# Attention ahead of two expert stages: a chunk's gate products from GpSimd to ScalarE, and a conversion's four small DMAs one step later

## The chip, the cores and the metric

The kernel runs on one core of one Trainium2 chip. The metric is the device time of one execution in microseconds (us); the kernel before took 919.73 us, the median of three runs (919.49 to 921.26). Engines are named as the profile names them: PE (TensorE matmul), PEld (its weight load), DVE (VectorE), ACT (ScalarE), POOL (GpSimd) and SP (SyncE, which here only issues DMAs). PEq, SPq and ACTq are the queues of PE, SP and ACT.

## What is computed

The program computes a gated linear attention, sends its output through a layer of eight experts with a fixed capacity, and that through a gated product with a third weight. The change lies in the attention, whose reference is, cut short:

```python
for t in range(S):                       # S = 768, B = 4, H = 8, D = 40
    m_new = np.maximum(f_gate[:, :, t] + m, i_gate[:, :, t])
    f_stab = np.exp(f_gate[:, :, t] + m - m_new)
    i_stab = np.exp(i_gate[:, :, t] - m_new)
    m = m_new
    C = f_stab * C + i_stab * outer(vt, kt)
    n = f_stab * n + i_stab * kt
    h_tilde = C @ qt
    y[:, :, t] = sigmoid(o_gate[:, :, t]) * h_tilde / max(abs(n . qt), 1)
x = y.transpose(0, 2, 1, 3).reshape(B * S, H * D)
x = moe(x)                               # 8 experts, 384 tokens each
out = (x @ w_a * (x @ w_b)) @ w_out
```

## The kernel before

The attention works in chunks of T = 128 tokens: NC = 6 chunks (c) by B = 4 batches (b) make 24 steps, n = 4c + b. In a step the queries and keys of eight heads are multiplied (`pq`, L392), and the result is weighted by a 128 x 128 matrix of decays per head. That matrix comes from one matmul per four heads, `pe` (L384): its stationary operand is `est[:, b]` (a row of the gates, kept only on the partitions of batch b) and its moving operand is `mov` (another row of the gates, kept only on the partitions of a head). ACT takes the exponential of `pe` into `dd` (L386), POOL clears what lies above the diagonal (L387, a select), DVE multiplies `pq` by `dd` into `P` (L395), and PE multiplies `P` by the values into `pv` (L423). POOL later forms `x` from numerator, denominator and output gate (L460, L462), PE transposes it (`px`, L472) and takes the routing logits (`pl`, L482). Everything is one program per engine, each in the order in which it was written: the function `attention` interleaves the pieces of neighbouring steps by hand, with generators. `s1(n + 1)` (the pe, dd, P part of the next step) runs inside step n; `pe` has one PSUM buffer, so the second half's `pe` waits for the first half's `dd`.

`gates(c)` makes a chunk's gate rows, and is run in small portions by `fill` during the chunk before (each `yield` ends a portion; after `yield "w"` the next generator in the list has its turn). In its last part POOL forms `mov` in two halves of four heads (L323, 128 x 512 each) and `est` in one (L332, 128 x 512), all as products of a row with a 0/1 column per head or batch, `hsel` and `bsel`. The first chunk has its own branch, before the loop. A step n is counted here by PE's time, from its first `pe` of `s1(n + 1)` to the next. By it the products of chunks 2 to 5 run in steps 5, 9, 13 and 17 (`mov` first half and `est`; the program writes them at the end of the step before) and in steps 6, 10, 14 and 18 (`mov` second half); those of chunk 1 run in step 2.

Beside the attention runs `conv`: 13 pieces of the last stage's weights are decoded from 64-bit words on DVE (`mu`, L119, L122, L125) and ACT (`mq`, `msg`), split into a high part on ACT (`wh` L131, `mth` L133, `woh` L148) and a low part on POOL (`wl` L134, `mtl` L136, `wol` L149). DVE's next piece waits for the low part, as `mu` has one buffer. A piece of kind "f" (nine of the 13) ends with four small DMAs on SP, from `mth` and `mtl` into `wh` (L139, L140). The function `fin` of a piece is put into a list and run by `flush`, once a step; DMAs that `self.dma` puts off (`x`'s store, the output gate's load) and the raw weights' loads are issued by `drain`, right after `flush`.

SP issues the loads of the step after next at the head of each step: four of `qr` (L263, L264; three buffers, so the load waits until the matmul `pg`, L408, of the step before has read the buffer) and one of `vk` (L266). Its queue is in order: a DMA that waits holds back all behind it.

Of the kernel before, what the change touches and what calls it, by code (L numbers as in the profile page):

```python
# [6 lines left out]
F32 = mybir.dt.float32  # L7
# [7 lines left out]
AF = mybir.ActivationFunctionType  # L15
# [5 lines left out]
B, H, S, D = 4, 8, 768, 40  # L21
# [22 lines left out]
class Kern:  # L44
# [68 lines left out]
    def conv(self, pool, kind, i, raw, more, nxt):  # L113
        nc = self.nc
        V, P, A = nc.vector, nc.gpsimd, nc.scalar
        words = raw.bitcast(I32).rearrange("p (n two) -> p n two", two=2)
        qi, sg = self.cva
        u = pool.tile([128, CW], I32, tag="ot", name="mu", bufs=1)
        V.tensor_scalar(u, words[:, :, 1], 3, None, op0=OP.logical_shift_left)  # L119
        more()  # L120
        yield 0.5
        V.tensor_tensor(u, u, qi, op=OP.add)  # L122
        yield 0.8
        F = u.bitcast(F32)
        V.tensor_tensor(F, F, sg, op=OP.mult)  # L125
        if kind == "f":
            h, l = self.wh[i], self.wl[i]
            n4, c4 = slice(0, 512), slice(512, 640)

            def fin():  # L130
                A.activation(h[:, 0:4].rearrange("p a b -> p (a b)"), F[:, n4], AF.Copy)  # L131
                th, tl = [pool.tile([128, 128], F32R, name=n, bufs=1) for n in ("mth", "mtl")]
                A.activation(th, F[:, c4], AF.Copy)  # L133
                P.tensor_sub(l.rearrange("p a b -> p (a b)"), F[:, n4],  # L134
                             h[:, 0:4].rearrange("p a b -> p (a b)").bitcast(F32))
                P.tensor_sub(tl, F[:, c4], th.bitcast(F32))  # L136
                for s in range(2):
                    r = slice(64 * s, 64 * s + 64)
                    nc.sync.dma_start(h[0:64, 4 + s].bitcast(F32), th[r].bitcast(F32))  # L139
                    nc.sync.dma_start(h[64:128, 4 + s].bitcast(F32), tl[r].bitcast(F32))  # L140
                nxt()

            yield from self.later(fin)
        else:
            h = self.woh[i].rearrange("p a b -> p (a b)")

            def fin():
                A.activation(h, F, AF.Copy)  # L148
                P.tensor_sub(self.wol[i].rearrange("p a b -> p (a b)"), F, h.bitcast(F32))  # L149
                nxt()  # L150

            yield from self.later(fin)
        self.done.add((kind, i))
# [60 lines left out]
    def attention(self, es):  # L214
        tc, nc, a = self.tc, self.nc, self.a
# [18 lines left out]
        hsel = gs[:, 6:14]  # L234
        dsel = gs[:, 14:30]
        psel = gs[:, 30:158]
        bsel = gs[:, 158:162]
# [36 lines left out]
        def sig(c):  # L274
            nc.scalar.activation(SG[c], SG[c], AF.Sigmoid)
            nc.scalar.activation(warm, gs[0:1, 0:1], AF.Exp)

        def gates(c):
            t = FI.pop(c)
            fg, ig = t[:, 0], t[:, 1]  # L280
            mt = wk.tile([128, 1 + T], F32, name="mt")
            if c:
                nc.vector.tensor_copy(mt[:, 0:1], MT[c - 1][:, T:])
            else:
                nc.vector.memset(mt[:, 0:1], -1e30)
            MT[c] = mt
            mc, mp = mt[:, 1:], mt[:, 0:T]
            yield 0
            nc.vector.tensor_tensor_scan(mc, fg, ig, mp[:, 0:1], op0=OP.add, op1=OP.max)
            yield 0  # L290
            lf = wk.tile([128, T], F32, name="lf", bufs=1)
            nc.vector.tensor_add(lf, fg, mp)
            yield 0
            nc.vector.tensor_sub(lf, lf, mc)
            if c == 0:
                nc.vector.memset(lf[:, 0:1], 0.0)
            yield 0
            cc = wk.tile([128, T], F32, name="cc", bufs=1)
            nc.vector.tensor_sub(cc, ig, mc)
            A = wk.tile([128, T], F32, name="A", bufs=1)  # L300
            nc.vector.tensor_tensor_scan(A, self.ones, lf, 0.0, op0=OP.mult, op1=OP.add)
            yield 0
            zs = wk.tile([128, 2, T], F32, name="zs", bufs=1)
            nc.vector.tensor_scalar(zs[:, 1], A, za, oa, op0=OP.mult, op1=OP.add)
            nc.vector.tensor_sub(cc, cc, A)
            yield 0
            nc.vector.tensor_scalar(zs[:, 0], cc, zc, oc, op0=OP.mult, op1=OP.add)
            hi = wk.tile([128, 2, T], F32R, name="hi", bufs=1)
            EW = wk.tile([128, 2, T], F32, name="EW", bufs=1)

            def fin():
                nc.scalar.activation(hi, zs, AF.Copy)
                nc.scalar.activation(EW[:, 0], A, AF.Exp)
                nc.scalar.activation(EW[:, 1], cc, AF.Exp, bias=A[:, T - 1:T])

            yield from self.later(fin, False)
            ar = wk.tile([128, T], F32, name="ar", bufs=1)
            nc.vector.scalar_tensor_tensor(ar, hi[:, 1].bitcast(F32), b2, zs[:, 1], op0=OP.mult, op1=OP.add)
            mov = wk.tile([128, H, T], F32R, name="mov")

            def half(g):
                e = nc.vector if c == 0 and g else nc.gpsimd
                e.tensor_tensor(mov[:, 4 * g:4 * g + 4], ar[:, None, :].to_broadcast([128, 4, T]),  # L323
                                hsel[:, 4 * g:4 * g + 4, None].to_broadcast([128, 4, T]), op=OP.mult)

            half(0)
            es1 = wk.tile([128, T], F32, name="es1", bufs=1)
            nc.vector.scalar_tensor_tensor(es1, hi[:, 0].bitcast(F32), b1, zs[:, 0], op0=OP.mult, op1=OP.add)
            est = wk.tile([128, B, T], F32R, name="est")

            def spread(e, b0, b1_):
                e.tensor_tensor(est[:, b0:b1_], es1[:, None, :].to_broadcast([128, b1_ - b0, T]),  # L332
                                bsel[:, b0:b1_, None].to_broadcast([128, b1_ - b0, T]), op=OP.mult)

            if c == 0:
                spread(nc.vector, 0, 1)
            else:
                spread(nc.gpsimd, 0, B)
            yield 0
            md = wk.tile([128, 16], F32, name="md", bufs=1)  # L340
            nc.vector.tensor_scalar(md, dsel, EW[:, 0, T - 1:T], None, op0=OP.mult)
            yield 0
            for _ in range(4):
                yield "w"
            half(1)
            if c == 0:
                spread(nc.gpsimd, 1, B)
            GA[c] = (est, mov, EW, md)
            yield 0

# [171 lines left out]
        for n in range(NS):  # L522
            c, b = divmod(n, B)
            if n == 2:
                bg.append(m2)
            if True:
                if n + 2 < NS:
                    load(n + 2)
                if n == 1:
                    next(m2)  # L530
                if b == 3 and c + 1 < NC:
                    gates2(c + 1)
                    if c + 2 < NC:
                        bg.insert(0, gates(c + 2))
                        if c + 3 < NC:
                            load_g(c + 3)
                m = s1(n + 1) if n + 1 < NS else iter(())
                next(m, None)
                g = s2g(n)
                next(g, None)  # L540
                fill(2)
                next(m, None)
                next(m, None)
                if n == 0:
                    sig(0)
                if b == 3 and c + 1 < NC:
                    sig(c + 1)
                self.flush(b < 3)
                self.drain()
                next(g, None)  # L550
                next(m, None)
                if n + 1 < NS:
                    pre(n + 1)
                g = s2(n)
                next(g)
                if 0 <= n - 2:
                    s3(n - 2)
                next(g)
                lc = s4(n - 3) if n >= 3 else lambda: None
                fill(2)  # L560
                next(g)
                fill(1)
                next(g)
                fill(1)
                next(g, None)
                lc()
            if n:
                xout(n - 1)
                if n % B == 0 and n // B + 1 < NC:
                    load_o(n // B + 1)  # L570
            if n - 3 == 7 or n - 3 == 15:
                bg.insert(0, self.keys(*KT[(n - 3) // 8]))
            fill(1)
# [643 lines left out]
```

## Time and profile before

| | us |
|---|---|
| median of three runs | 919.73 |
| the profiled execution | 922.35 |
| its span, first to last instruction | 920.6 |
| busy in the span: PE / PEld | 830.0 / 786.8 |
| busy in the span: DVE / POOL / ACT | 543.8 / 433.6 / 337.0 |

The profiled execution took 2.6 us more than the median. A row of a timeline gives the start, the duration, the engine, the line, the operation, the tile written and those read, and in brackets how long the engine was idle just before and what ended that. A releaser is inferred: it is the last thing that ended before the wait did. A mean share over the whole span says little here, since the attention (the first 212 us) and the two expert stages after it have different limits.

### The profile page before, as it was taken

The page shows a single profiled execution, that of the slowest core. Times are in us where ns is not written, and L with a number is a line of the kernel's source. Part 1 is how long each engine was busy: PE and PEld are TensorE (multiplying, and loading weights), DVE is VectorE, ACT ScalarE, POOL GpSimd, SP SyncE. Part 2 cuts the span into 40 slices and gives each one's busy share as a digit, 9 for nine tenths or more (in the row PEclk, how much of TensorE's full clock was granted, in tenths as well). Part 3 has the DMA queues.
Part 4 walks back from the last instruction along what each step waited for, and adds up shares of the span by engine and source line. Part 5 has one row for each costly group of instructions (what it writes and reads, how often), then busy time and mean ns, then how long its engine had stood idle before and what let it go on. Part 6 is the DMA issues. An engine that isn't in the chain of part 4 may idle for free.

```text
span 920.6 us, 15838 instructions
## 1 busy us (share of the span) xinstructions
PE 830.0 (90%) x5939; PEld 786.8 (85%) x5939; DVE 543.8 (59%) x1188; ACT 337.0 (37%) x660; POOL 433.6 (47%) x456
## 2 busy tenths in 40 slices
PE   4888978995878889979989999999999999999996
PEld 3788867884778879979988998999899999999996
DVE  7778996846676786585477678667764321321211
ACT  4657646520334332333234224223422532432321
POOL 5688895750433573165147317442723633532122
PEclk9989988896799889989998999999999999999999
DMA  6866765621412220130131022021111311200000
GB/s 170 246 193 198 238 199 143 199 75 41 147 51 72 80 79 22 53 84 13 38 89 45 15 80 75 2 94 32 46 52 43 92 36 43 67 8 22 1 1 22
DMA packets 51037, 73.84 MB, mean 80 GB/s; under 512 B 6160, under 2 KB 41360, under 8 KB 50960
## 3 DMA queue, kind: packets, MB, share of 16 engines
q1 hardware_dynamic: 41744, 45.30, 17.7%
q10 hardware_dynamic: 6912, 19.66, 6.6%
q0 software_dynamic: 2304, 7.87, 2.6%
q8 instruction: 47, 0.77, 0.3%
q14 instruction: 30, 0.25, 0.1%
HBM read 63.37 MB, written 7.86 MB: 77 GB/s over the span
## 4 chain that ended last, share of the span: by engine, by line
PE 64%; DVE 16%; POOL 6%; issue 6%; ACT 5%; DMA 2%; SPq 1%; ACTq 0%; DVEq 0%; POOLq 0%
PE ring L970 32%; PE acc L970 20%; DVE G L648 3%; PE rt L672 2%; PE pq L392 2%; DMA qr<-in_qk_dram 2%; PE pv L423 1%; DVE w1h L907 1%; POOL dd L387 1%; DVE gf L1093 1%; PE pg L408 1%; PE pl L482 1%; DVE mu L122 1%; POOL x L460 1%; ACT yh L966 1%
## 5 line engine op out<-in xcount | busy, mean ns | idle before, releaser
L1098 POOL TENSOR_TENSOR ml<-gf,mh 128x384 fp32r<-128x384 f32 x95 | 106.7, 1123 | 266.4 <-ACT mh L1095 266.1
L970 PE MATMUL ring<-yh,wh 128*128 128x384 f32 x576 | 202.3, 351 | 6.4 <-ACT yh L966 4.6
L970 PE MATMUL ring<-yl,wh 128*128 128x384 f32 x576 | 136.9, 344 | 0.0
L970 PE MATMUL ring<-yh,wl 128*128 128x384 f32 x384 | 132.7, 346 | 0.0
L1093 DVE TENSOR_TENSOR gf<-ring,at 128x384 f32<-128x384 f32 x96 | 53.3, 555 | 126.9 <-PE ring L970 122.8
L970 PEld LDWEIGHTS ring<-yh,wh 128*128 128x128 f32 x576 | 111.4, 193 | 13.9 <-ACT yh L966 7.2
L1095 ACT ACTIVATE mh<-gf 128x384 fp32r<-128x384 f32 x96 | 50.5, 526 | 187.0 <-DVE gf L1093 187.0
L648 DVE TENSOR_TENSOR G<-thc,d 128x1024 bf16<-128x1024 int16 (+1 forms) x90 | 110.4, 1245 | 0.4
L970 PEld LDWEIGHTS ring<-yl,wh 128*128 128x128 f32 x576 | 105.6, 193 | 0.1
L970 PE MATMUL acc<-woh,ml 128*128 128x320 f32 x288 | 91.6, 318 | 0.0
L970 PE MATMUL acc<-woh,mh 128*128 128x320 f32 x288 | 90.7, 315 | 0.0
L970 PE MATMUL acc<-wol,mh 128*128 128x320 f32 x288 | 90.4, 314 | 0.0
L970 PE MATMUL acc<-mh,w 128*128 128x384 f32 x320 | 88.9, 340 | 0.0
L1036 DVE SCALAR_TENSOR_TENSOR ml<-ring,mh 128x384 fp32r<-128x384 f32 x64 | 35.5, 557 | 80.3 <-ACT mh L1034 77.1
L1034 ACT ACTIVATE mh<-ring 128x384 fp32r<-128x384 f32 x64 | 31.5, 492 | 133.5 <-PE ring L970 128.9
L1091 ACT ACTIVATE at<-ring 128x384 f32<-128x384 f32 x96 | 46.8, 488 | 80.0 <-PE ring L970 78.3
L970 PEld LDWEIGHTS ring<-yh,wl 128*128 128x128 f32 x384 | 74.4, 194 | 0.0
L906 POOL TENSOR_TENSOR w1l<-raw,w1h 128x512 fp32r<-128x512 f32 x30 | 44.2, 1478 | 51.0 <-ACT w1h L902 51.0
L970 PE MATMUL ring<-xh,w1h 128*128 128x384 f32 x192 | 66.0, 344 | 0.1
L392 PE MATMUL pq<-qr 128*128 128x256 f32 x192 | 56.9, 425 | 9.9 <-DMA qr<-in_qk_dram 5.2
L970 PE MATMUL acc<-ml,w 128*128 128x384 f32 x192 | 65.2, 339 | 0.3 <-DVE ml L1036 0.3
L970 PEld LDWEIGHTS acc<-mh,w 128*128 128x128 f32 x320 | 58.6, 190 | 0.2 <-issue 0.2
(211 smaller groups left out, 1746.8 us busy)
## 6 DMA issues: line engine op xcount, KB each, us to landing
raw<-in_moe_w_dram SPq DMA_DIRECT2D x32, 320.0 KB
raw<-in_moe_w_dram SPq DMA_DIRECT2D x32, 256.0 KB
vk<-in_vk_dram SPq DMA_DIRECT2D x24, 324.0 KB
qr<-in_qk_dram SPq DMA_DIRECT2D x48, 160.0 KB
mraw<-in_wab_dram ACTq DMA_DIRECT2D x12, 640.0 KB
raw<-in_moe_w_dram SPq DMA_DIRECT2D x64, 64.0 KB
og<-in_og_dram ACTq DMA_DIRECT2D x6, 640.0 KB
qr<-in_qk_dram SPq DMA_DIRECT2D x48, 80.0 KB
```

The costliest lines, as they stand in the source:

```text
L122: V.tensor_tensor(u, u, qi, op=OP.add)
L392: nc.tensor.matmul(pq[:, o:o + 2], qk[:, 4 + hp], qk[:, H + 2 * hp:H + 2 * hp + 2], start=True, stop=True)
L648: self.nc.vector.tensor_tensor(G, self.thc[:, None, 0:nthr].to_broadcast(dims), d[:, i0:i0 + 8, None].to_broadcast(dims), op=op)
L672: nc.tensor.matmul(cnt[0:nthr], Gs[j][:, i], oh[:, 8 * j + i], start=(j + i == 0), stop=(j * 8 + i == NT - 1))
L906: e.tensor_sub(l, raw[:, 0:2], h[:, 0:2].bitcast(F32))
L970: self.nc.tensor.matmul(*a, **k)
L1034: A.activation(hh, p, AF.Relu)
L1036: V.scalar_tensor_tensor(hl, p, 0.0, hh.bitcast(F32), op0=OP.max, op1=OP.subtract)
L1091: A.activation(at, p[0], AF.Copy)
L1093: V.tensor_mul(gf, p[1], at)
L1095: A.activation(gh, gf, AF.Copy)
L1098: e.tensor_sub(gl, gf, gh.bitcast(F32))
```

## The change

In chunks 1 to 5 the products leave POOL. ACT makes them as 12 copies of 128 x 128, each scaled by a column per partition (`bsel` or `hsel`): four for `est`, eight for `mov`, three in each of four portions. The four small DMAs of a conversion piece are no longer issued by `fin` but put off, to the `drain` of the next step. And `drain` now stands ahead of `flush` in a step.

```diff
--- before.py
+++ after.py
@@ -134,10 +134,14 @@
                 P.tensor_sub(l.rearrange("p a b -> p (a b)"), F[:, n4],
                              h[:, 0:4].rearrange("p a b -> p (a b)").bitcast(F32))
                 P.tensor_sub(tl, F[:, c4], th.bitcast(F32))
-                for s in range(2):
-                    r = slice(64 * s, 64 * s + 64)
-                    nc.sync.dma_start(h[0:64, 4 + s].bitcast(F32), th[r].bitcast(F32))
-                    nc.sync.dma_start(h[64:128, 4 + s].bitcast(F32), tl[r].bitcast(F32))
+
+                def pieces():
+                    for s in range(2):
+                        r = slice(64 * s, 64 * s + 64)
+                        nc.sync.dma_start(h[0:64, 4 + s].bitcast(F32), th[r].bitcast(F32))
+                        nc.sync.dma_start(h[64:128, 4 + s].bitcast(F32), tl[r].bitcast(F32))
+
+                self.dma(pieces)
                 nxt()
 
             yield from self.later(fin)
@@ -323,7 +327,8 @@
                 e.tensor_tensor(mov[:, 4 * g:4 * g + 4], ar[:, None, :].to_broadcast([128, 4, T]),
                                 hsel[:, 4 * g:4 * g + 4, None].to_broadcast([128, 4, T]), op=OP.mult)
 
-            half(0)
+            if c == 0:
+                half(0)
             es1 = wk.tile([128, T], F32, name="es1", bufs=1)
             nc.vector.scalar_tensor_tensor(es1, hi[:, 0].bitcast(F32), b1, zs[:, 0], op0=OP.mult, op1=OP.add)
             est = wk.tile([128, B, T], F32R, name="est")
@@ -334,17 +339,25 @@
 
             if c == 0:
                 spread(nc.vector, 0, 1)
-            else:
-                spread(nc.gpsimd, 0, B)
             yield 0
             md = wk.tile([128, 16], F32, name="md", bufs=1)
             nc.vector.tensor_scalar(md, dsel, EW[:, 0, T - 1:T], None, op0=OP.mult)
             yield 0
-            for _ in range(4):
+            if c == 0:
+                half(1)
+                spread(nc.gpsimd, 1, B)
+            else:
+                def scaled(i0, i1):
+                    for i in range(i0, i1):
+                        if i < B:
+                            nc.scalar.activation(est[:, i], es1, AF.Copy, scale=bsel[:, i:i + 1])
+                        else:
+                            nc.scalar.activation(mov[:, i - B], ar, AF.Copy, scale=hsel[:, i - B:i - B + 1])
+
                 yield "w"
-            half(1)
-            if c == 0:
-                spread(nc.gpsimd, 1, B)
+                for i in range(0, 12, 3):
+                    scaled(i, i + 3)
+                    yield "w"
             GA[c] = (est, mov, EW, md)
             yield 0
 
@@ -545,8 +558,8 @@
                     sig(0)
                 if b == 3 and c + 1 < NC:
                     sig(c + 1)
+                self.drain()
                 self.flush(b < 3)
-                self.drain()
                 next(g, None)
                 next(m, None)
                 if n + 1 < NS:
```

What this does to the order on three engines, by rows of the two programs (line numbers of the changed one are higher).

ACT, around the exponentials (`dd`) of step 5, where the products of chunk 2 are made, and on to the split of the next piece. Before:

```order
L475 ACTIVATE xt_135<-px 64x128
L386 ACTIVATE dd<-pe 128x512 x2
L447 ACTIVATE Cb<-Cc 40x4x41 x2
L131 ACTIVATE wh_71<-mu 128x512
L133 ACTIVATE mth<-mu 128x128
L110 DMA mraw<-in_wab_dram 128x640
L188 ACTIVATE mq<-mraw 128x640
L190 ACTIVATE msg<-mraw 128x640
L465 DMA xd<-x 128x320
L272 DMA og<-in_og_dram 128x1280
```

Now:

```order
L488 ACTIVATE xt_135<-px 64x128
L353 ACTIVATE est<-es_653,gs 128x128 x4
L355 ACTIVATE mov<-ar,gs 128x128 x2
L399 ACTIVATE dd<-pe 128x512
L355 ACTIVATE mov<-ar,gs 128x128 x3
L399 ACTIVATE dd<-pe 128x512
L478 DMA xd<-x 128x320
L276 DMA og<-in_og_dram 128x1280
L110 DMA mraw<-in_wab_dram 128x640
L460 ACTIVATE Cb<-Cc 40x4x41 x2
L131 ACTIVATE wh_71<-mu 128x512
L133 ACTIVATE mth<-mu 128x128
```

Six copies stand ahead of the first `dd`, three between the two (the last three stand ahead of the next step's first `dd`), and the DMA issues have moved from behind the split to ahead of `Cb` and `wh`.

SP, the first piece's four DMAs and the loads around them. Before:

```order
L266 DMA vk<-in_vk_dram 128x648
L139 DMA wh_69<-mth 64x128
L140 DMA wh_69<-mtl 64x128
L139 DMA wh_69<-mth 64x128
L140 DMA wh_69<-mtl 64x128
L263 DMA qr_127<-in_qk_dram 40x1024
L264 DMA qr_127<-in_qk_dram 40x4x128
L263 DMA qr_127<-in_qk_dram 40x1024
L264 DMA qr_127<-in_qk_dram 40x4x128
L266 DMA vk<-in_vk_dram 128x648
L139 DMA wh_71<-mth 64x128
```

Now:

```order
L270 DMA vk<-in_vk_dram 128x648
L267 DMA qr_127<-in_qk_dram 40x1024
L268 DMA qr_127<-in_qk_dram 40x4x128
L267 DMA qr_127<-in_qk_dram 40x1024
L268 DMA qr_127<-in_qk_dram 40x4x128
L270 DMA vk<-in_vk_dram 128x648
L141 DMA wh_69<-mth 64x128
L142 DMA wh_69<-mtl 64x128
L141 DMA wh_69<-mth 64x128
L142 DMA wh_69<-mtl 64x128
L267 DMA qr_128<-in_qk_dram 40x1024
```

The loads of a step have passed the four DMAs of the piece that was split in the step before.

POOL, the step in which the products of chunk 2 were made. Before:

```order
L368 TENSOR_TENSOR wv<-vk,gt 128x328
L373 TENSOR_TENSOR ct<-Cc,gt 128x164
L323 TENSOR_TENSOR mov<-ar,gs 128x512
L332 TENSOR_TENSOR est<-es_649,gs 128x512
L460 TENSOR_TENSOR x<-num,den 128x320
L462 TENSOR_TENSOR x<-x,og 128x320
L387 AFFINE_SELECT dd<-dd 128x512 x2
L134 TENSOR_TENSOR wl_72<-mu,wh_71 128x512
```

Now:

```order
L381 TENSOR_TENSOR wv<-vk,gt 128x328
L386 TENSOR_TENSOR ct<-Cc,gt 128x164
L473 TENSOR_TENSOR x<-num,den 128x320
L475 TENSOR_TENSOR x<-x,og 128x320
L400 AFFINE_SELECT dd<-dd 128x512 x2
L134 TENSOR_TENSOR wl_72<-mu,wh_71 128x512
```

Two of the three products stood between `ct` and `x` here; the third stood in the same place of the next step.

## Rows read from the trace of the kernel before

**Rows 1.** Windows by stage: busy PE, PEld, DVE, ACT, POOL; PEclk, DMA share, GB/s.

```profile
25.90:211.90 186.00, 162.36 (x1285) 147.33 (x1284) 139.24 (x318) 104.13 (x219) 136.50 (x160) 0.91 0.63 182
211.90:920.60 708.70, 656.13 (x4596) 630.32 (x4594) 386.69 (x823) 222.35 (x426) 283.94 (x272) 0.95 0.17 50
```

**Rows 2.** Timeline of PE: the first `pe` of steps 9 to 12, 15 and 16.

```profile
83.14 0.48 PE L384 MATMUL pe<-mov,est 128*128 128x512 f32 x1
...
93.27 0.77 PE L384 MATMUL pe<-mov,est 128*128 128x512 f32 x1
...
101.34 0.48 PE L384 MATMUL pe<-mov,est 128*128 128x512 f32 x1
...
107.76 0.48 PE L384 MATMUL pe<-mov,est 128*128 128x512 f32 x1
...
135.84 0.77 PE L384 MATMUL pe<-mov,est 128*128 128x512 f32 x1
...
147.01 0.48 PE L384 MATMUL pe<-mov,est 128*128 128x512 f32 x1
```

**Rows 3.** Timeline of step 9, in which the products of chunk 3 are made.

```profile
83.97 0.59 ACT L386 ACTIVATE dd<-pe 128x512 f32<-128x512 f32 x1
...
85.11 1.04 POOL L323 TENSOR_TENSOR mov<-ar,gs 128x512 fp32r<-128x512 f32 x1
86.11 1.70 POOL L332 TENSOR_TENSOR est<-es,gs 128x512 fp32r<-128x512 f32 x1
...
89.97 1.22 POOL L387 TENSOR_SCALAR_AFFINE_SELECT dd<-dd 128x512 f32<-128x512 f32 x2
...
87.01 1.48 DVE L125 TENSOR_TENSOR mu<-mu,msg 128x640 f32<-128x640 f32 x1
90.64 0.69 DVE L395 TENSOR_TENSOR P<-pq,dd 128x512 f32<-128x512 f32 x1 [2.15 <-PE px L472]
```

**Rows 4.** Timeline of DVE in steps 9 and 10.

```profile
86.09 0.81 DVE L122 CUSTOM_DVE_ANT_0 mu<-mu,mq 128x1280 uint16<-128x1280 uint16 x1
...
94.23 1.67 DVE L122 CUSTOM_DVE_ANT_0 mu<-mu,mq 128x1280 uint16<-128x1280 uint16 x1
...
98.71 0.69 DVE L395 TENSOR_TENSOR P<-pq,dd 128x512 f32<-128x512 f32 x1 [0.39 <-POOL dd L387]
```

**Rows 5.** Timeline of POOL and DVE: the halves of steps 10, 13 and 2.

```profile
94.18 1.04 POOL L323 TENSOR_TENSOR mov<-ar,gs 128x512 fp32r<-128x512 f32 x1
...
123.39 0.68 DVE L395 TENSOR_TENSOR P<-pq,dd 128x512 f32<-128x512 f32 x1
...
34.99 0.64 POOL L387 TENSOR_SCALAR_AFFINE_SELECT dd<-dd 128x512 f32<-128x512 f32 x1 [0.82 <-ACT dd L386]
```

**Rows 6.** Timeline of ACT: a 128 x 128 activation with a column operand, and the next.

```profile
81.09 0.39 ACT L314 ACTIVATE EW<-cc,A 128x128 f32<-128x128 f32 x1
81.38 0.61 ACT L131 ACTIVATE wh<-mu 128x512 fp32r<-128x512 f32 x1
```

**Rows 7.** Waits of SP's queue in the attention: us in total, times, longest.

```profile
SPq L139 <- ACT mth L133: 28.9, 8, 6.1
SPq L140 <- POOL mtl L136: 15.0, 9, 3.0
```

**Rows 8.** Timeline of PE and SP around the release and the load of one buffer.

```profile
77.42 1.02 PE L408 MATMUL pg<-Cb,qr 128*128 128x82 f32 x8
...
85.64 0.46 SPq L263 DMA_DIRECT2D qr<-in_qk_dram  x1
```

**Rows 9.** Timeline: two late loads, and the raw weights' DMA beside the first.

```profile
131.35 0.34 ACTq L110 DMA_DIRECT2D mraw<-in_wab_dram  x1
...
131.56 0.28 SPq L264 DMA_DIRECT2D qr<-in_qk_dram  x1
...
138.98 2.04 PE L392 MATMUL pq<-qr 128*128 128x256 f32 x4 [2.37 <-DVE mt L283]
...
196.28 1.10 PE L392 MATMUL pq<-qr 128*128 128x256 f32 x4 [1.94 <-DMA qr<-in_qk_dram]
```

## The prediction, made before the changed kernel ran

> **What bounds the kernel now.** I read the windows by stage first: the attention takes 186 us of the span and the expert stages the other 709; PE is busy 162.4 us of the 186 in the attention, DVE 139.2, POOL 136.5, ACT 104.1, the DMA engines 63% [rows 1]. No engine is full there, so the stage is bound by what waits for what. What comes after starts from the last routing logits, so a microsecond won in the attention is one won at the end; the expert stages hold no changed instruction.
>
> Next I read PE's timeline for the length of single steps. Step 11, which makes no products, takes 107.76 - 101.34 = 6.42 us; step 9, which makes them, 93.27 - 83.14 = 10.13; step 10, with the second half of `mov`, 8.07; step 15 takes 147.01 - 135.84 = 11.17 though it has the same place in its chunk as step 11 [rows 2]. What the long ones have in excess is where the change must pay.
>
> Step 9: the first `dd` leaves ACT at 84.56, but POOL, in order, first does `mov` (85.11, 1.04 us), `est` (86.11, 1.70) and `x`, and comes to the selects at 89.97; DVE, done with `mu` at 88.49, stands idle 2.15 us before `P` [rows 3]. The row names PE's `px` as releaser, but `P` needs POOL's selects, and these ended when it started. Step 10: `P` is idle only 0.39 us [rows 4], but DVE is held earlier: its L122 takes 1.67 us there against 0.81 in step 9 [rows 4], and starts 0.05 us after POOL's `mov` half of 1.04 us [rows 5].
>
> Step 15: PE stands 2.37 us before `pq` at 138.98 [rows 9]. The row names a DVE copy, which PE doesn't read; its `qr` load was issued at 131.56, and `pq`'s PSUM buffer was long free, so I read it as the load. The waits of SP's queue say why loads are late: its first small DMA waited 28.9 us in all for `mth`, its second 15.0 us for `mtl` [rows 7], with the next loads behind. In one case the buffer's last reader `pg` ended at 78.44 and the load went out at 85.64, behind four small DMAs [rows 8]: 7.2 us lost.
>
> **Part one, the products.** POOL loses three operations per chunk, five times. In steps 9, and 5 and 17, which are like it, `P` can come forward by DVE's idle 2.15 us (POOL gives 1.04 + 1.70 = 2.74, so DVE is next). In the step after, 0.39 plus 1.67 - 0.81 = 0.86 is to be had, if L122 was held by POOL: 1.25. Together at most 3.4 per chunk.
>
> That L122 was held by `mov` is read from two starts 0.05 us apart and two durations; by 0.39 alone the step after would give 0.9 less. The Trainium skill (SBUF — State Buffer, section Who interferes with whom) says that VectorE and GpSimd share one pair of ports as an exclusive lock and that the one that came second blocks fully; the rows agree (the loser's 1.67 is longer than 0.81 by nearly the winner's 1.04). By that rule the two steps give 3.4, without it 2.5.
>
> ACT pays. No row shows a scaled copy; the nearest is the exponential of 128 x 128 with a column as bias, 0.39 us long, with the next operation starting 0.29 us after it [rows 6]. So 12 copies hold ACT for 3.5 us per chunk; were each its full 0.39 us, 4.7. Six stand ahead of the first `dd`: it ends 6 x 0.29 = 1.7 us later, at 86.3 instead of 84.56, which still lies under POOL's `x`, at whose end the select can start (89.97 - 2.74 = 87.23) [rows 3]. The second `dd` follows after three copies (0.87) and its own 0.59, near 87.8: the selects then end near 88.5, as two of them take 1.22 [rows 3]. What no longer hides is what stands behind: three copies (0.87) and one DMA issue (0.34 [rows 9]) push the split `wh`, for which POOL's `wl` and then DVE's next `mu` wait: 1.2 us back. I take 3.4 - 1.2 = 2.2 for chunks 2, 3 and 5. For chunk 4 DVE had no idle time before `P` in step 13 [rows 5] (it builds routing keys there), so only the step after is sure: 1.3, with 0 and 3.4 as ends. For chunk 1 POOL was waiting 0.82 us for ACT's `dd` already [rows 5]; up to 0.87 can be lost there (three copies ahead of it) and up to 1.0 won: 0. Sum of the part: 3 x 2.2 + 1.3 = **7.9 us**.
>
> **Part two, the small DMAs.** They cost what they did, but now stand behind the next step's loads, and wait for an `mtl` that is done or nearly so. The loads go out when `pg` releases the buffer, up to 7.2 us sooner [rows 8]. The next `mth` and `mtl` must wait until the earlier ones are read, but these DMAs could not leave before `mtl` anyway, so that wait is where it was: 0. Waits that this ends: step 15, between 2.37 us (the idle time alone) and 4.75 (its excess over step 11, since the following matmuls ran slower, too); I take 3.5. And 1.94 us before `pq` at 196.28 [rows 9]. Sum: **5.4 us**.
>
> **Part three, `drain` ahead of `flush`.** The store of `x` and the weight loads are now issued on ACT's queue ahead of `Cb` and the split. Where `x` is not done, ACT waits for POOL there, with `Cb`, `hi`, `wh` and the next `dd` behind. An issue is 0.34 us [rows 9], and most of a pair hides under the `dd` just started (0.59 [rows 3]). The 13 splits stand behind two issues each now; the cost is between 0 (all hidden) and 13 x 0.68 = 8.8 us; I take 2.0, six issues, nearer to nothing, because a pair outlasts that `dd` by only 0.1 us.
>
> Sum: 7.9 + 5.4 - 2.0 = 11.3. Against the profiled execution that is 922.35 - 11.3 = 911.0; it lies 2.6 above the median of 919.73, against which the time is compared: **908.4 us**.
>
> **Rivals.** (a) ACT takes POOL's place: the copies and the issues ahead of the split eat the products' gain, and only the loads pay: 919.7 - 5.4 + 2.0 = 916.3. For it: ACT's queue had 12 entries put in front of `dd`. Against: ACT is the least busy of the four engines [rows 1]. Chance 0.17.
>
> (b) The loads go out sooner but land no sooner, since the DMA engines are the limit: 919.7 - 7.9 + 2.0 = 913.8. For it: the load issued at 131.56 took 7.4 us to be used, beside a 640 KB weight load issued at 131.35 [rows 9]. Against: 63% of the DMA engines' time on average [rows 1]. The Trainium skill (DMA: Bandwidth & Descriptors, section Issuing engines are not separate DMA queues) says that DMAs of all issuing engines run on the same 16 engines and interleave; by that rule the weight load, which also goes out sooner now, keeps sharing with `qr`, and the result is this case. Chance 0.13.
>
> (c) Slower: ACT becomes what ends last in the steps with products. The place is the first `dd`, behind six copies; it decides from the point at which that `dd` ends later than POOL gets to its select (by the sum above 86.3 against 87.2, so 0.9 us away). Then POOL's relief is worth nothing, all 12 copies are added, 5 x 3.5 = 17.4, and with the loads' gain and the issues 919.7 + 17.4 - 5.4 + 2.0 = 933.7. Chance 0.06.
>
> (d) The change does nothing that counts: the next waiter (DVE's chain through `mu`) takes all: 919.7. Chance 0.05.
>
> **How the numbers follow.** The forecast has 0.59. Its best end: 3 x 3.4 + 3.4 + 1.0 for the products, 4.75 + 1.94 for the loads, nothing for the issues: 21.3, or 898.4. About 0.2% (1.8 us) is what a measurement can tell from no change. Faster by more: 0.59 + 0.17 + 0.13, less a hundredth for their bad ends: 0.88; within: 0.05; slower: 0.07. A range from 899 to 917 holds the forecast, (a) and (b), and leaves out about 0.15.
>
> **What would show it.** In the profile after: POOL's busy time lower by 17 to 18 us in the attention, ACT's higher by about 5 x 12 x 0.39 = 23 with overlaps counted twice; `P`'s idle time in steps 5, 9 and 17 under 0.7 us, and those steps near 8 us; SP's loads right behind `pg`, with no `mth` or `mtl` wait between; step 15 under 8 us; the end of the attention near 200 instead of 211.9. It is wrong if POOL's selects wait for `dd` in those steps, if ACT stands idle before the store of `x` with `Cb` behind it, or if `pq` still waits for `qr`.

## The result, and the profile after

| | before | after |
|---|---|---|
| median of six runs, us | 919.75 | 910.0 |
| lowest and highest, us | 917.26, 921.43 | 908.33, 914.87 |
| the profiled execution, us | 922.35 | 908.33 |
| its span, us | 920.6 | 906.6 |
| ACT / POOL busy in the span, us | 337.0 / 433.6 | 353.3 / 415.9 |

The ratio of after to before is 0.9901, 95% interval 0.9872 to 0.9929: 9 us faster (6.5 to 12). The forecast was 908.4, the range 899 to 917.

The windows by stage of after (busy PE, PEld, DVE, ACT, POOL; granted clock, DMA share, GB/s), beside [rows 1]:

```profile
25.90:196.60 170.70, 152.47 (x1285) 139.34 (x1284) 134.23 (x318) 121.16 (x279) 119.56 (x145) 0.97 0.67 199
196.60:906.60 710.00, 658.59 (x4596) 632.20 (x4594) 386.30 (x823) 221.62 (x426) 283.16 (x272) 0.95 0.17 50
```

The window that holds the same 318 DVE and 1285 PE instructions is 15.3 us shorter; POOL has lost 15 operations and 16.9 us, ACT won 60 and 17.0 us (23 were put down, at 0.39 us each with overlaps counted twice). The expert stages are 1.3 us longer in this execution; I read nothing into that.

Steps, each from its first `pe` to the next one's, in the two profiled executions:

| step | 5 | 6 | 9 | 10 | 13 | 14 | 15 | 17 | 18 |
|---|---|---|---|---|---|---|---|---|---|
| before, us | 11.33 | 8.05 | 10.13 | 8.07 | 8.44 | 12.39 | 11.17 | 9.38 | 10.40 |
| after, us | 7.67 | 10.54 | 7.67 | 9.66 | 10.37 | 7.27 | 6.42 | 7.68 | 10.07 |

PE's timeline of after, the first `pe` of steps 9 to 12, 15 and 16, beside [rows 2]:

```profile
82.50 0.48 PE L397 MATMUL pe<-mov,est 128*128 128x512 f32 x1
...
90.17 0.48 PE L397 MATMUL pe<-mov,est 128*128 128x512 f32 x1
...
99.83 0.48 PE L397 MATMUL pe<-mov,est 128*128 128x512 f32 x1
106.25 0.48 PE L397 MATMUL pe<-mov,est 128*128 128x512 f32 x1
...
124.07 0.47 PE L397 MATMUL pe<-mov,est 128*128 128x512 f32 x1
...
131.34 0.48 PE L397 MATMUL pe<-mov,est 128*128 128x512 f32 x1
```

Steps 5, 9 and 17, with `est` and the first half of `mov`, gave what was forecast or about it, and so did step 15. But steps 6 and 10, with the second half, grew by 2.5 and 1.6 us. In chunk 4 the gain came the other way round: step 13 grew by 1.9, step 14 fell by 5.1, together 3.2 us won where 1.3 was put down. Why it fell out so there was not followed further. From the last `pe` row's step on (its start at 193.85 before, 182.40 after) to the first routing matmul it is 18.35 us before and 14.52 after. The nine steps of the table win 12.0 us, this tail 3.8; the other steps lose 0.6.

The timeline of after in steps 9 and 10 (start, duration, engine, line, operation; in brackets the idle time before and its inferred end), beside [rows 3, 4]:

```profile
83.35 1.26 ACT L353 ACTIVATE est<-es,gs 128x128 fp32r<-128x128 f32 x4
84.52 0.68 ACT L355 ACTIVATE mov<-ar,gs 128x128 fp32r<-128x128 f32 x2
...
86.45 0.57 ACT L399 ACTIVATE dd<-pe 128x512 f32<-128x512 f32 x1
86.70 0.33 ACTq L478 DMA_DIRECT2D xd<-x  x1
87.07 0.44 ACTq L276 DMA_DIRECT2D og<-in_og_dram  x1
87.63 0.38 ACTq L110 DMA_DIRECT2D mraw<-in_wab_dram  x1
88.06 0.69 ACT L460 ACTIVATE Cb<-Cc 40x164 f32<-40x164 f32 x2 [1.04 <-POOL dd L400]
...
94.68 0.33 ACTq L478 DMA_DIRECT2D xd<-x  x1
95.67 0.33 ACTq L110 DMA_DIRECT2D mraw<-in_wab_dram  x1
96.05 0.69 ACT L460 ACTIVATE Cb<-Cc 40x164 f32<-40x164 f32 x2 [2.00 <-DVE mu L125]
...
86.62 1.81 POOL L400 TENSOR_SCALAR_AFFINE_SELECT dd<-dd 128x512 f32<-128x512 f32 x2
89.50 1.28 POOL L134 TENSOR_TENSOR wl<-mu,wh 128x512 fp32r<-128x512 f32 x1 [1.06 <-ACT wh L131]
...
92.53 0.72 POOL L473 TENSOR_TENSOR x<-num,den 128x320 f32<-128x320 f32 x1
93.32 1.33 POOL L475 TENSOR_TENSOR x<-x,og 128x320 f32<-128x320 f32 x1
...
87.88 0.69 DVE L408 TENSOR_TENSOR P<-pq,dd 128x512 f32<-128x512 f32 x1 [0.53 <-POOL dd L400]
...
92.58 1.35 DVE L122 CUSTOM_DVE_ANT_0 mu<-mu,mq 128x1280 uint16<-128x1280 uint16 x1
...
99.42 0.44 PE L368 MATMUL pgt<-identf,EW 128*128 128x128 f32 x2 [1.82 <-ACT xt L488]
```

Step 9 goes as reasoned: the copies start 0.29 us apart (four of them in 84.52 - 83.35), the selects begin 4.12 us into the step instead of 6.83 [rows 2, 3], and `P` is idle 0.53 us instead of 2.15. What is new stands between a `dd` and `Cb` (ACT's copy of the state `Cc`, which the next `pg` reads). In step 9 three issues follow each other, without a wait between them, and ACT is idle 1.04 us for their own time. In step 10 the last `dd` ended at 94.06; the store waits until `x` ends at 94.65, and the weight load then waits again until 95.67 (for what, the built programs under e8 say), so `Cb` comes 2.00 us late. The releasers in the brackets are not the cause: `Cb`'s data were done. All behind is late: `wh`, for which POOL's `wl` stands idle, and `xt`, for which the transposes of `gates2` (`pgt`, the first work of step 11 on PE) wait.

The waits of after in the attention (us in total, times, longest):

```profile
POOL wl L134 <- ACT wh L131: 11.8, 8, 2.2
DVE mu L119 <- POOL mtl L136: 10.5, 7, 2.7
PE pgt L368 <- ACT xt L488: 6.0, 4, 2.3
...
SPq L270 <- PE pst L442: 36.1, 17, 5.3
SPq L267 <- PE pg L421: 14.2, 5, 5.7
SPq L142 <- POOL mtl L136: 2.2, 5, 0.6
```

SP now waits above all for the buffers' readers, and hardly for `mtl` any more: 2.2 us, against the 15.0 of [rows 7].

### The profile page after: what moved, and what is told of

Same layout as the page of the kernel before. It is cut to its first block, busy times and chain, and to the rows that moved or that the text cites. A ratio compares the mean times of both kernels' runs of the same rounds, so it can differ in the third digit from the quotient of the medians.

```text
span 906.6 us, 15898 instructions
## 1 busy us (share of the span) xinstructions
PE 822.6 (91%) x5939; PEld 780.7 (86%) x5939; DVE 538.4 (59%) x1188; ACT 353.3 (39%) x720; POOL 415.9 (46%) x441
## 3 DMA queue, kind: packets, MB, share of 16 engines
q0 software_dynamic: 2304, 7.87, 2.7%
## 4 chain that ended last, share of the span: by engine, by line
PE 66%; DVE 15%; ACT 7%; issue 4%; DMA 4%; POOL 2%; SPq 0%; ACTq 0%; DVEq 0%; POOLq 0%
PE ring L983 33%; PE acc L983 20%; DVE G L661 4%; PE pq L405 2%; PE rt L685 2%; PE pv L436 2%; DVE w1h L920 1%; DMA qr<-in_qk_dram 1%; PE pl L495 1%; DMA vk<-in_vk_dram 1%; DVE gf L1106 1%; PE pe L397 1%; PE pg L421 1%; DMA mraw<-in_wab_dram 1%; ACT yh L979 1%
## 5 line engine op out<-in xcount | busy, mean ns | idle before, releaser
L983 PEld LDWEIGHTS acc<-woh,mh 128*128 128x128 f32 x288 | 55.1, 191 | 2.6 <-issue 2.6
```

What stands on the lines that cost most here:

```text
L983: self.nc.tensor.matmul(*a, **k)
```

## The experiments

All twelve, with the start of the first routing matmul in the profiled execution as the attention's end (212.20 before, 196.92 after). The runs of before beside them had medians of 919.87, 918.52 and 920.86 us in the three series.

| run | median, us | ratio to before, 95% | attention's end |
|---|---|---|---|
| e1 copies only | 911.89 | 0.9922 (0.9886 to 0.9958) | 201.79 |
| e2 small DMAs late only | 915.11 | 0.9955 (0.9924 to 0.9985) | 204.03 |
| e3 drain first only | 924.03 | 1.0042 (1.0016 to 1.0069) | 209.50 |
| e4 change, issues behind flush | 899.97 | 0.9785 (0.9750 to 0.9819) | 190.30 |
| e6 store ahead | 915.11 | 0.9959 (0.9935 to 0.9983) | 203.30 |
| e7 weights ahead | 910.24 | 0.9911 (0.9879 to 0.9944) | 200.23 |
| e8 store behind xt | 909.56 | 0.9884 (0.9844 to 0.9923) | 201.90 |
| e9 second half on GpSimd | 903.00 | 0.9843 (0.9800 to 0.9886) | 192.51 |
| e11 e8 plus one DMA | 901.64 | 0.9797 (0.9753 to 0.9840) | 189.47 |
| e12 e7 plus one DMA | 911.96 | 0.9902 (0.9872 to 0.9932) | 200.30 |
| e13 gate load on SP | 907.61 | 0.9873 (0.9828 to 0.9917) | 195.92 |
| e15 gate load a step later | 923.07 | 1.0029 (1.0004 to 1.0054) | 212.69 |

**e1, the copies alone.** From the changed kernel, two edits undone:

```diff
-                self.dma(pieces)
+                for s in range(2):
...
-                self.drain()
                 self.flush(b < 3)
+                self.drain()
```

> The products as ScalarE copies alone; the four small DMAs and the order of flush and drain as before. Theory A (copies and loads both pay, the issues ahead of the split eat some of it): the steps 5, 9 and 17 shrink to about 7.7 us as in the changed kernel, step 15 stays above 10 us, the late wait for qr stays; 910 to 914 us. Rival B (nearly all comes from the loads): 917 to 920 us. Rival C (the longer steps 6, 10 and 18 are the copies' own work on ScalarE): these steps stay at 9.7 us or more here too; 914 to 916 us. By A they fall back to about 8 to 9 us.

By the ratio 7.2 us are won: A's size. But the steps don't fit A: 5, 9 and 17 fall to 7.68, 7.66 and 7.67 as it says, while 6 and 10 grow to 11.72 and 10.81, more than in the changed kernel, and step 15, which was to stay above 10 us, falls to 8.06. C calls the long steps the copies' own work; e4 below has the same copies, and there these steps are 8.57 us. ACT's timeline in step 10 of this run:

```profile
97.78 0.74 ACT L148 ACTIVATE woh<-mu 128x640 fp32r<-128x640 f32 x1
100.52 0.34 ACTq L110 DMA_DIRECT2D mraw<-in_wab_dram  x1
100.91 0.92 ACT L188 ACTIVATE mq<-mraw 128x640 uint16<-128x640 uint32 x1 [2.38 <-DMA qr<-in_qk_dram]
```

ACT stands still behind a weight load that is not issued until a load of `qr`, another queue's, has landed.

**e2, the small DMAs alone.** From the kernel before, with the pieces' DMAs in a list `sq` of their own:

```diff
-                for s in range(2):
...
+                self.dma(pieces, self.sq)
...
+                self.drain(self.sq)
                 self.flush(b < 3)
                 self.drain()
```

> Only the four small DMAs go one step later (issued ahead of flush, from a list of their own); the store of x and the weight loads stay behind flush, the products stay on GpSimd. Theory A: step 15 falls to about 6.5 us and the wait for qr near 196 us goes; 911 to 914 us. Rival B: 909 to 911 us, nearly the whole gain of the change. If the loads land no sooner because the DMA engines are the limit: 918 to 920 us, with step 15 still above 10 us.

4 us are won; by the interval 1.4 to 7.0. The median lies just over A's range, and step 15 falls from 11.17 to 8.42 us only, not to 6.5. Rival B, that this part pays nearly all, is out.

**e3, drain first alone.** From the kernel before:

```diff
-                self.flush(b < 3)
                 self.drain()
+                self.flush(b < 3)
```

> Only drain ahead of flush: the store of x and the weight loads are issued on ScalarE's queue ahead of Cb and the split; the small DMAs are issued with the split as before, the products stay on GpSimd. Theory A: slower, 922 to 926 us, with ScalarE idle 1 us or more before Cb in most steps and GpSimd waiting more for wh. Rival C (drain ahead of flush costs nothing): 918.5 to 921 us. Rival D (the earlier weight loads and stores pay): 915 to 918 us.

Slower, as A says, by 3.9 us (1.5 to 6.3). Its waits of ACT (`Cb`'s were 5.5 us in all before):

```profile
ACT Cb L447 <- DVE P L395: 17.9, 4, 5.6
ACT Cb L447 <- DVE L L483: 10.0, 4, 4.4
```

Where the 3.9 us go this trace doesn't show: in the profiled execution, at 921.65 us below the median, the attention ends 2.7 us earlier than before, in spite of these waits. And step 15 fell to 6.42 us here, with the small DMAs still where they were, as it fell to 8.06 in e1. So their place is not the only thing that made that step long.

**e4, the change with only the small DMAs ahead of `flush`.**

```diff
-                self.drain()
+                self.drain(self.sq)
                 self.flush(b < 3)
+                self.drain()
```

> The changed kernel, but only the small DMAs are issued ahead of flush; the store of x and the weight loads are issued behind it, as before. Theory A: faster than the changed kernel by 3 to 6 us, 904 to 907 us; the steps 6, 10 and 18 fall to about 8 to 9 us and ScalarE no longer stands idle 1 to 2 us before Cb. Rival C: 909 to 911 us, no difference. Rival D: slower than the changed kernel, 912 to 915 us.

900.0 us, 10 less than the changed kernel and more than the two parts' own gains together (7.2 + 4.1). Steps 6, 10 and 18 are 8.57, 8.57 and 7.87; `pgt` waits 1.0 us in all for `xt` instead of 6.0. That is below A's range too; rivals C and D are out: taking the issues back behind `flush` is what wins. In the profiled executions 6.6 of it are won by the end of the attention; 2.8 lie in the expert stages, which hold no changed instruction, and are not explained. Which of the issues it is, the next two ask.

**e6 and e7, one kind of issue at a time.** e6 drains `dq` (the store, the gate's load, the pieces) ahead of `flush` and `rq` (the weight loads) behind it; e7 `sq` and `rq` ahead, `dq` behind:

```diff
-                self.drain()
+                self.drain(self.dq)
                 self.flush(b < 3)
+                self.drain(self.rq)
```

> The changed kernel, but only the weight loads go back behind flush; the store of x, the output gate's load and the small DMAs are still issued ahead of it. Theory X (the store of x is the price: it waits for GpSimd's x, with Cb, the split and xt behind it on ScalarE): 906 to 911 us, little better than the changed kernel, ScalarE still idle 1 us or more before Cb. Theory W (the weight loads are the price, each waiting for an earlier transfer or a buffer): 899 to 902 us. Both half: 904 to 906 us.

> The changed kernel, but only the store of x and the output gate's load go back behind flush; the weight loads and the small DMAs are still issued ahead of it. Theory X: 899 to 903 us, no idle time before Cb that ends with GpSimd's x. Theory W: 906 to 911 us, with Cb behind the weight loads. Both half: 904 to 906 us.

Neither theory fits both: e7's time is W's, but by W e6 should have been fast, and it is slower than X says. Either kind alone loses all that e4 had won, and e6 loses more. The waits of ACT in e7 name the place:

```profile
ACT xt L487 <- DMA mraw<-in_wab_dram: 11.8, 4, 3.3
```

`xt` doesn't read `mraw`. What stands ahead of it on ACT is the issue of the output gate's load, so that issue waits for a weight load to land.

**e8, the store behind `xt`.** e4 with `drain(self.rq)` behind `flush` and `drain(self.dq)` after the call of `s3`, ahead of `s4`.

> The variant with the issues behind flush, and the store of x and the output gate's load moved further back on ScalarE's queue, behind the copy of px into xt. If what stands behind a store that waits for GpSimd is what pays, xt no longer waits (1.2 us in two places there, and 1.5 us once for an earlier store): 897 to 899.5 us. If those waits are covered: 899.5 to 901 us. If a later load of the output gate or a later store of x is missed: over 901.5 us.

10 us slower than e4, on an edit that only moves issues to where nothing should wait; the third case has the number, but not the cause. Step 6 takes 13.73 us. ACT's timeline there:

```profile
57.53 0.34 ACTq L110 DMA_DIRECT2D mraw<-in_wab_dram  x1
...
59.88 0.26 ACT L488 ACTIVATE xt<-px 64x128 f32<-64x128 f32 x1
63.32 0.34 ACTq L276 DMA_DIRECT2D og<-in_og_dram  x1
63.71 0.99 ACT L355 ACTIVATE mov<-ar,gs 128x128 fp32r<-128x128 f32 x3 [3.57 <-DMA mraw<-in_wab_dram]
```

The built programs (each engine's instructions with their semaphores, as they go to the chip) say what couples them. A semaphore is a counter that a DMA raises as it lands. The DMAs of SP's and ACT's queues take eight semaphores in turn, in the order of the built program, and an issue waits until the DMA that used its semaphore eight places earlier has landed. The place of a DMA in that order, its queue and semaphore, and what used it before, for e8, for e11 below, and for step 10 of the changed kernel and of e6:

```
e8    62 ACT mraw  sem 6   before: 54 SP wh (a small DMA)
e8    70 ACT og    sem 6   before: 62 ACT mraw
e11   63 ACT mraw  sem 7   before: 55 ACT xd
e11   70 ACT og    sem 6   before: 62 SP qr
e11   71 SP  wh    sem 7   before: 63 ACT mraw
after 112 ACT mraw sem 0   before: 104 SP wh (a small DMA)
e6    112 ACT xd   sem 0   before: 104 SP wh (a small DMA)
```

The traces hold the times at which the semaphores rise. In e8 the weight load raises semaphore 6 for the last time at 63.30, and the gate's load goes out at 63.32. In step 10 of the changed kernel the small DMA, issued at 90.08, is done at 95.57, and the weight load goes out at 95.67: the change has put that DMA eight places ahead of it. In e6 it is the store that stands there: done at 96.92, issued at 97.00, with ACT idle 3.26 us before `Cb`.

**e11 and e12, one element more.** A DMA of one element ahead of the gate's load, in e8 and in e7; the rows of all five engines are otherwise in the same order.

```diff
+                if c > 1:
+                    nc.sync.dma_start(one.tile([1, 1], F32, name=f"dum{c}"), a["gsel"][0:1, 0:1])
                 nc.scalar.dma_start(o_, a["og"][:, c])
```

> The variant with the store of x behind xt, with nothing moved, and four bytes more: one DMA of a single element on SP ahead of each output gate's load of chunks 3 to 6. In the built program the DMAs of SP's and ScalarE's queues take eight semaphores in turn, and an issue waits until the transfer that used its semaphore before, eight places earlier, has landed. Without the added DMA the output gate's load stands eight places behind a 640 KB weight load, and ScalarE waits 2 to 3.6 us for that landing, four times; with it, it stands behind a load of qr. Theory L (these landings are the price): 899 to 903 us, with no wait of ScalarE that ends with mraw. Theory N (the transfers themselves are the price): no faster than without, 908 to 911 us.

> The variant with the weight loads ahead of flush and the store of x behind it, with the same added DMA of one element. There too the output gate's load stood eight places behind a weight load (11.8 us of ScalarE's waits in four places). Theory L: 899 to 903 us, so the weight loads' place ahead of flush costs little by itself and what is left of the changed kernel's loss belongs to the store of x and the landings that it waits for. Theory N: 908 to 911 us. If the weight loads' place itself costs half: 904 to 906 us.

e11 shows it: theory L's time, with four bytes more to move and 8 us less (901.64 against 909.56; the ratios' intervals don't meet, but only just: 0.9844 and up for e8, 0.9840 and down for e11). No wait of ACT ends with `mraw` any more (11.1 us in four places in e8); a small DMA on SP's queue waits for those landings instead, 3.0 us in three places. Steps 6, 10 and 18 are 7.85, 7.83 and 7.84. The Trainium skill asks for one semaphore per slot in flight, as a wait on a shared one can pass before the data has landed (DMA: Bandwidth & Descriptors, section Why a DMA increments its semaphore by 16 and not by 1). These programs get by with eight, by making the ninth issue wait, and the rows show what that takes on a queue that also computes.

e12 wins nothing: its 911.96 us lie past N's range, though its gate's load is free as well. There the next weight load, ahead of `Cb`, has come to stand eight places behind a small DMA and waits for that to land:

```profile
96.92 0.60 ACT L405 ACTIVATE dd<-pe 128x512 f32<-128x512 f32 x1 [0.96 <-PE pe L403]
101.27 0.34 ACTq L110 DMA_DIRECT2D mraw<-in_wab_dram  x1
101.66 0.34 ACT L466 ACTIVATE Cb<-Cc 40x164 f32<-40x164 f32 x1 [4.13 <-DMA wh<-mtl]
```

So e12 moved the wait instead of removing it, and what the weight loads' place ahead of `flush` would cost without any landing stays open.

**e13, the gate's load on SP.** e4 with `nc.sync` in place of `nc.scalar` for chunks 2 to 5 (the expectations of e11, e13 and e15 count the chunks from one).

> The variant with the issues behind flush, but the output gate's loads of chunks 3 to 6 are issued by SP instead of ScalarE. If ScalarE's own issue and what stands behind it is still worth something (0.44 us each and xt behind): 897 to 899.5 us. If that is covered: 899.5 to 902 us. If SP's queue, waiting there for the last reader of the buffer, brings qr's loads late: over 903 us.

The third case by its time: ACT's `mq` waits 3.4 us in three places for loads of `qr`, and steps 7 and 11 are 8.07 and 7.61 us. `mq` doesn't read `qr` either: as in e1, the weight load ahead of it stands eight places behind a load of `qr` in the built program.

**e15, the gate's load a step later.** e4 with `n % B == 1 and n > B` as the condition of that load.

> The variant with the issues behind flush, but the output gate's loads of chunks 3 to 6 are written one step later, so that they don't go out between two weight loads. If too many bytes at once are what still lengthens the steps 6, 10 and 18 (8.57, 8.57 and 7.87 us against 6.42 in step 7): 895 to 898 us. If the landing of some other transfer then takes the place: 899 to 903 us. If the gate comes too late for its sigmoid at the chunk's last step: over 903 us.

A little slower than the kernel before, and not for the reason given: PE stands still ahead of `pgt`, 20.9 us in four places.

```profile
106.37 0.11 DVE L496 TENSOR_SCALAR L<-pl 128x8 f32<-128x8 f32 x1
...
106.54 0.69 PE L368 MATMUL pgt<-identf,EW 128*128 128x128 f32 x2 [5.18 <-DVE L L496]
```

In the built program of e15 `pgt` waits for DVE, where in e4 it waits for PE and ACT: the three tiles that share two PSUM buffers (`px`, `pl`, `pgt`) fell the other way round. The question about bytes was not answered.

**e9, the second half back on POOL.** e4 with copies 0 to 7 only, then `half(1)`.

> The variant with the issues behind flush, but the second half of mov stays on GpSimd, as one product in the steps 6, 10, 14 and 18 as before the change; est and the first half are still ScalarE copies. If the second half's move won what the prediction put on it (1.25 us in each of four or five chunks): 904 to 907 us. If it won nothing, because DVE's L122 still meets another GpSimd product there: 899 to 902 us. If ScalarE's copies are what lengthens these steps (8.57 us against 8.05 before): 896 to 899 us.

903.0 us, an end of the attention 2.2 us later than e4's, with intervals that overlap: between the first two cases. DVE's timeline in step 10 of e9, where `mov` meets it again:

```profile
88.98 1.67 DVE L122 CUSTOM_DVE_ANT_0 mu<-mu,mq 128x1280 uint16<-128x1280 uint16 x1
```

## Why the prediction was right, and where its terms were wrong

The time, the sign and the range held: 11.3 us forecast, 9 measured. That the time came so near is luck: the first two parts together give more than was forecast (20 us in e4, not 13.3), the third takes more (10, not 2), and these errors cancelled.

**Part one, the products: 7.9 forecast, 7.2 alone (e1; 3.9 to 10.5).** Step 9 was right row by row: the first `dd` ends 3.2 us into the step, as 86.3 - 83.14 said, `P`'s idle time fell to 0.53 us, and `wl` stands idle 1.06 us behind the late `wh` where 1.2 was put down. Wrong was the step after, "0.39 plus 1.67 - 0.81 = 0.86". L122 did not fall to 0.81 but to 1.35 in chunks 2 to 5: POOL, freed of `mov`, does `x` at that moment, and its product of 0.72 us holds L122 for 0.54. So 0.32 of 0.86 was won there; e9 shows 1.67 again where `mov` is back. That one holds the other was right; that something else of POOL's would move into the slot was not asked. These three durations (0.81 alone, 1.35 beside 0.72, 1.67 beside 1.04) agree with the lock on the shared ports that the Trainium skill describes (SBUF — State Buffer, section Who interferes with whom).

That e1's total is the forecast's is luck as well. In its profiled execution steps 5 and 6 together, and 9 and 10, won nothing (19.40 and 18.47 us against 19.38 and 18.20 before), where 2.2 each was put down; 13 and 14 won 2.9, 17 and 18 won 3.7, and step 15, which the sum has under the loads, 3.1. In e4, with the issues behind `flush`, the four pairs won 3.2, 2.0, 3.8 and 4.2: 13.1 us, near the part's best end.

**Part two, the loads: 5.4 forecast, 4 alone (e2; 1.4 to 7.0).** Step 15 fell to 6.42 us and the tail by 3.8, as forecast or better, but not by the small DMAs' place alone: e2 brings step 15 to 8.42, and e1 and e3, which leave them, to 8.06 and 6.42. The waits of SP's queue before, of which [rows 7] shows two, had more:

```profile
SPq L266 <- DMA mraw<-in_wab_dram: 13.1, 3, 5.8
...
SPq L264 <- DMA wh<-mtl: 3.0, 3, 1.6
```

L266 loads `vk`, which has nothing to do with `mraw`, and L264 loads `qr`, which has nothing to do with `wh`. I passed over these rows. In the built program of before exactly three loads of `vk` stand eight places behind a weight load. And the load of `qr` that step 15 waits for (issued at 131.56 [rows 9]) stands eight places behind a small DMA that was issued at 125.95 and is done at 131.54. It then needs until 138.89 itself; the weight load beside it is done at 138.30. Each variant changes both the pairs and the times of the transfers, so what share of step 15's fall belongs to which is not shown.

**Part three, the issues: 2.0 forecast, 3.9 alone (e3) and 10 beside the other two (after against e4).** This is the step that failed. It priced an issue by its own 0.34 us and hid pairs of them under a `dd`. What an issue costs is what it waits for: `x` on POOL, and the landing eight places earlier, and everything behind it on ACT: 2 to 4 us at a time (2.00 in step 10 of the changed kernel, 3.26 in e6, 4.13 in e12). "Wrong if ACT stands idle before `x`'s store with `Cb` behind it" was named as a sign and did appear. The upper bound of 8.8 us, made of issue times, is passed by the medians; the two intervals leave room for 7 to 15 us. How much of the 10 is the place of the issues, and how much the pairs that e4 happens to have, is open: e12, meant for that, only moved the wait.

**The sum.** 7.9 + 5.4 - 2.0 came within 2 us because what was missing had opposite signs, as said above. That the first two together give more than 7.2 + 4.1 fits the landings: in e1 ACT runs into them (`mq` waits 6.5 us for loads of `qr`), in e4 hardly (`xt` waits 1.5 us once for a store and 0.4 once for `qr`). That is argued and not tested. Which landing meets which issue in the changed kernel was read from step 10 only.

**The rivals.** (a) is out: without the copies e2 gives 4 us, with them e4 gives 20. (b) is out as put, since step 15 and the tail got shorter. That DMAs of two queues hold each other up came true by a semaphore; whether bytes do it too is open, as the load issued at 131.56 took 7.3 us to land and e15 did not settle it. (c) is out: the selects never waited for `dd` in step 9, and the spacing of the copies was the 0.29 us taken from [rows 6].

**What beats both:** e4, 900.0 us, 2.2% under the kernel before (1.8 to 2.5); e11 can't be told from it.

## What to carry to other kernels

On an engine that both computes and issues DMAs, the place of an issue is the place of a wait: ask what that issue waits for (its data, its buffer, and the transfer whose semaphore it takes over), and keep it behind the work that others wait for. When a row names a transfer that the waiting instruction has nothing to do with, believe it, and look in the built program for the semaphore. An edit that adds or moves one DMA re-deals these pairs for all that follow, so a variant that is slower than it should be may only have drawn a worse hand: e11 shows how to find out.

## What was not expected of the hardware

A copy scaled by a column holds ACT as long as the exponential with a column as bias [rows 6]: 0.29 us to the next start. And the mean granted clock of the attention was 0.91 before [rows 1] and 0.97 after, where PE had less idle time (18.2 us of the window instead of 23.6); PE's same 1285 instructions were busy 152.5 us instead of 162.4. The first `pe` of steps 10 and 15 shows it: 0.77 us in [rows 2], 0.48 after. How much of the 15.3 us this makes, and how much the waits themselves, no run here separates.
